# Products of the state with w_in as three float32r passes over split parts, two heads in halves of the array's rows

## The chip, the cores and the metric

One core of a Trainium2 chip. The metric is the device time of the kernel in microseconds (us), the median of several executions. Five engines matter here: PE (TensorE, matrix products; its weight loads are listed apart as PEld), ACT (ScalarE), DVE (VectorE), POOL (GpSimd) and SP, whose queue issues the transfers.

## The reference, cut to what matters

All tensors are float32.

```
x (8, 8, 512, 64), state (8, 8, 32, 64), w_in (512, 2048), w_out (2048, 512)
xread = softmax(x @ state^T / 8) @ state            # tokens read the state
sread = softmax(state @ x^T / 8) @ x                # the state reads tokens
X = concat(xread, sread) -> rows of batch and token, columns of head and D
h = X @ w_in ; g = max(0.01 h, h) ; Y = g @ w_out   # first feed-forward
out = (silu(Y @ w_gate) * (Y @ w_val)) @ w_out2     # second feed-forward
```

The kernel never forms xread. With A the softmax over the state, `xread @ w_in = A @ (state @ w_in)`, where the product in brackets is made per head: D = 64 rows of w_in belong to one head, so a tile of 128 rows holds a pair of heads. It is small, and it is needed before the first h.

## The kernel before, in words

The input weights arrive as 64-bit words and are converted to float32 in a **conversion** (`convert`, L236) that goes over 32 tiles of 128x512: 16 of w_in (key "in", g, k: column block g of 512, row block k, which is also the pair of heads) and 16 of w_out (key "out", f), in the order ORDER. One tile takes four chunks, each of which is one letter `c` of the scripts below; chunks of neighbouring tiles interleave. In an iteration for tile k the chunks are: (1) ACT `scale` of k, the ACT half of the split of tile k-2 (`finish1_h`, L1051), `limit` of k-1; (2) ACT `low` and DVE `sign` of k; (3) DVE `join` of k-1; (4) the DVE half of the split of k-2 (`finish1_l`, L1058), `add` of k-1, the load of a further tile, and a store of the tile k-1 to DRAM if it is one of w_in. `limit` and `add` are on DVE for the first four tiles and on POOL for the others. A **split** (L164 to L168) cuts a float32 tile into a float32r part h (ACT) and the rest l (DVE), so that a product at float32 accuracy is three fast passes, l*h, h*l and h*h (`passes`, L440). Before the change only w_out tiles are split here; a w_in tile is complete after its `add`, one iteration earlier.

Three things read a w_in tile. `product_sw` (L464): the pair's 64-row halves, two full float32 matmuls into two PSUM banks, with four batches of the state (`flat`) stationary; two ACT copies (L478) bring the banks to SBUF and two transfers store them, for the later batches. There are 32 of these, each a letter `p`. `state_win` (L455): batch 0 alone, 64 zero-padded columns of `states` per pair, two float32 matmuls into two halves of one bank, which are then split (`keep_sw_h`, `keep_sw_l`) for h at once. There are 8 of these; two are the letters `h` of START. The third reader is the store.

Work order is written out by hand, and each engine takes its instructions in that order. START is the script up to the first h: letters 0 and 1 step the two softmax chains of batch 0, s and S place the state (ACT copies, L1230), c is a chunk, p a product if a tile is ready, h and l the state_win of batch 0, m the first `h_mm`. SLOT0 has a script for each of the 16 slots of batch 0: in a slot there is one `h_mm` (6 matmuls), one `y_mm` (12 matmuls), some c and some p. From batch 1 on nothing of the conversion of w_in is left.

```
START = "spc0Scpccc0p0cpccpcc1ccchcc1cccpc1clcpp0hcccpclp1c01cpcmcc"
```

The PSUM banks of products: in START four of the pool ps_y; in SLOT0 the two banks a and b, one each, so that a second product in a row waits for the ACT copies of the first. `pump_until(key)` (L294) runs chunks until a tile is ready.

Of the kernel before, what the change touches and what calls it, by code (L numbers as in the profile page):

```python
# [25 lines left out]
def kernel(  # L26
# [39 lines left out]
    P = 128  # L66
# [141 lines left out]
    def to_f32(key):  # L208

        engine = nc.gpsimd if key[0] in ("in", "out") and key not in keys1[:4] else nc.vector  # L210
# [3 lines left out]
        v = raw[key].bitcast(I32)  # L214
        return {
# [20 lines left out]
    def convert(keys, room, prepare, load_next, finish=None):  # L236
# [4 lines left out]
        while todo or before or (finish and done):  # L241
# [209 lines left out]
    WO = {}  # L451
    products = []
    sw_ps, SW_raw, SW = {}, {}, {}
# [569 lines left out]
    with tc.manual_schedule():  # L1023
# [15 lines left out]
        pair = [None]  # L1039

        def place1(key):

            if key[0] == "in":
                n, half = divmod(KD * key[1] + key[2], 2)
                if half == 0:
                    pair[0] = wres.tile([P, 2, 512], F32, tag=f"wr{n + NF1 // 2}", name="w_in")
                raw[key] = pair[0][:, half, :]
            else:
                raw[key] = cv.tile([P, 512], F32, tag="raw", name="raw", bufs=4)

        def finish1_h(key):  # L1051
            while any((KD * g + p) // 2 + NF1 // 2 == key[1] for g, p, _ in products):
                pump_products(1)
            t = wres.tile([P, 2, 512], F32R, tag=f"wr{key[1]}", name="w_parts")
            WO[key[1]] = (t[:, 0, :], t[:, 1, :])
            split_h(t[:, 0, :], raw[key])

        def finish1_l(key):  # L1058
            split_l(WO[key[1]][1], raw.pop(key), WO[key[1]][0])

# [113 lines left out]
        def keep_steps(g, q):  # L1174
            def product():
                pump_until(("in", g, 2 * q + 1))
                keep_sw_h(g, q, state_win(0, g, q, "b"))
# [36 lines left out]
        flat = cv.tile([P, NPAIR, B, NS], F32, name="flat")  # L1214
# [9 lines left out]
        nc.gpsimd.memset(states, 0.0)  # L1224
        make_identity(nc, ident)
# [11 lines left out]
        for action in START:  # L1237
# [6 lines left out]
            elif action == "h":  # L1244
                keep_sw_h(*keep[0], state_win(0, *keep.pop(0), "y"))
# [4 lines left out]
            elif action == "S":  # L1250
                place_states(slice(1, B))
            elif action in "mM":
# [10 lines left out]
        for g, q in keep:  # L1263
            pump_until(("in", g, 2 * q + 1))
            keep_sw_h(g, q, state_win(0, g, q, "y"))
# [218 lines left out]
```

## Time and profile before

| | us |
|---|---|
| median of 3 runs (lowest to highest) | 1473.97 (1473.49 to 1474.21) |
| the profiled execution's own time | 1474.32 |
| its span in the trace | 1472.5 |
| PE busy in the span | 1445.5 |
| ACT busy / DVE busy | 688.4 / 817.5 |

The span starts with the first instruction and ends with the last; the execution's own time is 1.8 us more. Times in the rows are counted from the start of the span. In a list in order of time a row gives the start, the length, the engine, the line, the operation and its tiles, how many were merged, and in square brackets the idle time of the engine before it with what ended it.

### The profile page before, as it was taken

How to read it: one execution, taken by the hardware profiler on the slowest of the kernel's cores; microseconds unless marked ns; L12 is line 12 of the kernel's file. 1: busy time of each engine (PE TensorE's matmuls, PEld its weight loads, DVE VectorE, ACT ScalarE, POOL GpSimd, SP SyncE). 2: the span in 40 equal slices, each digit the busy share in tenths (PEclk: the TensorE clock that was granted, in tenths of full speed). 3: DMA queues.
4: the chain of work that ended last, by engine and by line, in shares of the span. 5: the costliest groups of instructions: out<-in, count | busy, mean ns of one | idle time of the engine just before them, and what ended most of it. 6: DMA issues, size and time to landing. Idle time of an engine off the chain costs nothing.

```text
span 1472.5 us, 20781 instructions
## 1 busy us (share of the span) xinstructions
PE 1445.5 (98%) x7530; PEld 1154.0 (78%) x7530; DVE 817.5 (56%) x1420; ACT 688.4 (47%) x1243; POOL 67.6 (5%) x64
## 2 busy tenths in 40 slices
PE   5989999999999999999999999999999999999998
PEld 1445777777777778888888888888888888988887
DVE  5666578676767676343444535455344555544442
ACT  5887556565656666444333423334233343333322
POOL 1565000000000000000000000000000000000000
PEclk9999999999999999999999999999999999999999
DMA  8886546666665655260668676667766397876345
GB/s 281 292 291 232 182 175 240 201 224 207 215 221 178 240 185 208 94 208 18 217 195 278 223 233 210 194 215 242 236 196 193 103 316 245 266 250 193 117 151 192
DMA packets 145766, 307.57 MB, mean 209 GB/s; under 512 B 14080, under 2 KB 34816, under 8 KB 144640
## 3 DMA queue, kind: packets, MB, share of 16 engines
q1 hardware_dynamic: 144368, 297.72, 61.6%
q10 hardware_dynamic: 1296, 8.52, 1.4%
q8 instruction: 60, 0.98, 0.3%
q14 instruction: 42, 0.34, 0.1%
HBM read 231.74 MB, written 74.45 MB: 208 GB/s over the span
## 4 chain that ended last, share of the span: by engine, by line
PE 93%; DMA 2%; ACT 2%; DVE 1%; issue 1%; POOL 0%; SPq 0%; ACTq 0%; POOLq 0%
PE ps_y L446 23%; PE ps_o L446 18%; PE ps_x L733 18%; PE ps_h L446 13%; PE ps_s L733 9%; PE ps_a L733 4%; PE ps_t L446 2%; PE ps_sw L470 2%; PE ps_yt L446 2%; PE ps_s L321 1%; DMA ws<-in_dram 1%; ACT sw L478 1%; PE ps_r L418 1%; DMA wo<-wo 1%; PE ps_a L404 0%
## 5 line engine op out<-in xcount | busy, mean ns | idle before, releaser
L446 PE MATMUL ps_y<-gh,w_parts 128*128 128x512 f32 x1024 | 339.3, 391 | 0.0
L733 PE MATMUL ps_x<-yc,wq 128*128 128x512 f32 x1152 | 278.0, 389 | 0.0
L733 PEld LDWEIGHTS ps_x<-yc,wq 128*128 128x128 f32 x1152 | 216.2, 188 | 44.8
L446 PE MATMUL ps_o<-wo,zh 128*128 128x512 f32 x768 | 236.4, 389 | 0.0
L446 PEld LDWEIGHTS ps_y<-gh,w_parts 128*128 128x128 f32 x1024 | 192.2, 188 | 51.6 <-issue 9.1
L446 PE MATMUL ps_y<-gl,w_parts 128*128 128x512 f32 x512 | 199.3, 389 | 0.0
L168 DVE TENSOR_TENSOR gl<-hs,gh 128x512 fp32r<-128x512 f32 (+1 forms) x144 | 99.2, 689 | 144.2 <-ACT gh L165 142.6
L446 PEld LDWEIGHTS ps_o<-wo,zh 128*128 128x128 f32 x768 | 144.1, 188 | 29.9
L541 ACT ACTIVATE hs<-ps_h 128x512 f32<-128x512 f32 (+1 forms) x144 | 82.6, 574 | 172.9 <-PE ps_h L446 169.1
L446 PE MATMUL ps_o<-wo,zl 128*128 128x512 f32 x384 | 149.5, 389 | 0.3 <-DMA wo<-wo 0.3
L733 PE MATMUL ps_s<-yc,wq 128*128 128x512 f32 x576 | 146.1, 389 | 0.0
L168 DVE TENSOR_TENSOR zl<-z,zh 128x512 fp32r<-128x512 f32 x96 | 66.3, 691 | 114.4 <-ACT zh L165 114.4
L733 PEld LDWEIGHTS ps_s<-yc,wq 128*128 128x128 f32 x576 | 108.1, 188 | 22.5
L165 ACT CAST zh<-z 128x512 fp32r<-128x512 f32 x96 | 59.3, 622 | 140.4 <-PE ps_o L446 140.3
L753 ACT ACTIVATE sg<-C 128x512 f32<-128x512 f32 x72 | 45.5, 632 | 158.2 <-DVE C L749 158.2
L446 PEld LDWEIGHTS ps_y<-gl,w_parts 128*128 128x128 f32 x512 | 96.2, 188 | 19.6
L446 PE MATMUL ps_h<-ah,swl 128*128 128x512 f32 x256 | 106.2, 415 | 1.6 <-DVE swl L168 1.5
L749 DVE TENSOR_TENSOR C<-ps_s,C 128x512 f32<-128x512 f32 x48 | 33.2, 691 | 123.3 <-PE ps_s L733 123.2
L446 PE MATMUL ps_h<-al,swh 128*128 128x512 f32 x256 | 100.2, 391 | 0.4 <-DVE al L168 0.4
L745 ACT COPY C<-ps_x 128x512 f32<-128x512 f32 x96 | 55.9, 583 | 94.6 <-PE ps_x L733 94.6
L446 PE MATMUL ps_h<-ah,swh 128*128 128x512 f32 x256 | 100.1, 391 | 0.0
L165 ACT CAST gh<-hs 128x512 fp32r<-128x512 f32 (+1 forms) x144 | 85.6, 594 | 3.0
(131 smaller groups left out, 1958.6 us busy)
## 6 DMA issues: line engine op xcount, KB each, us to landing
wo<-wo SPq DMA_DIRECT2D x96, 512.0 KB
wq<-quad_gate SPq DMA_DIRECT2D x168, 256.0 KB
wq<-quad_val SPq DMA_DIRECT2D x168, 256.0 KB
ws<-in_dram SPq DMA_DIRECT2D x68, 512.0 KB
sw<-sw_dram SPq DMA_DIRECT2D x56, 256.0 KB
quad_gate<-hl SPq DMA_DIRECT2D x24, 512.0 KB
quad_val<-hl SPq DMA_DIRECT2D x24, 512.0 KB
yr<-y_dram SPq DMA_DIRECT2D x34, 256.0 KB
```

Of the source, the lines that this page charges most:

```text
L165: nc.scalar.copy(dst, src)
L168: nc.vector.tensor_tensor(out=dst, in0=src, in1=hi.bitcast(F32), op=ALU.subtract)
L321: nc.tensor.matmul(ps[2 * NS * i:2 * NS * (i + 1)], lhsT=states[:, p, b, :], rhs=xt.pop((b, p)), start=True, stop=True,)
L418: nc.tensor.matmul(ps[NS * k:NS * (k + 1), i], lhsT=v["et"][:, n:n + NS], rhs=tokens[i][:, c, NS * k:NS * (k + 1)], start=(c == 0), stop=( ...
L446: nc.tensor.matmul(ps, lhsT=w, rhs=v, start=first and n == 0, stop=last and n == len(todo) - 1)
L470: nc.tensor.matmul(ps[e], lhsT=flat[half, p, 4 * bs:4 * bs + 4, :].rearrange("d b n -> d (b n)"), rhs=raw["in", g, p][half], start=True, s ...
L478: nc.scalar.copy(t, ps[e])
L541: nc.scalar.activation(hs, ps[:, :n], AF.Prelu, alpha=0.01)
L733: nc.tensor.matmul(bank, lhsT=a, rhs=v, start=first and n == 0, stop=last and n == len(todo) - 1, skip_group_check=True,)
L745: nc.scalar.copy(t[0], src)
L749: nc.vector.tensor_tensor(out=kept[0], in0=bank, in1=kept[0], op=ALU.add)
L753: nc.scalar.activation(t[0], c, AF.Sigmoid)
```

## The change

Each w_in tile is now split too. The converted float32 tile stays in one of four rotating buffers (`raw`, formerly only for w_out); its parts go to `WIN`, in places that w_out parts or an output tile use later (`places`), and before such a place is taken over, `clear` runs the products that still read it. A w_in tile is therefore ready one iteration of four chunks later, and `pump_until` stands before the `h` letters. The scripts START and SLOT0 are the same. The state is split as well (`split_states`, run at the letter S after the copies of the state): ACT half and DVE half of 128x1024, then 16 POOL copies of 64x32 into zero-padded columns for state_win, whose tile POOL clears at the start. `state_win` becomes six float32r matmuls over 128 rows and 128 columns; `product_sw` three pairs of float32r matmuls, the two 64-row halves alternating. Left out of the diff: a moved line and the tile allocations of `flat`.

```diff
                 load_next()
-                if not finish or before[0] == "in":
+                store(before)
+                if not finish:
                     ready.append(before)
-                    store(before)
...
-    def state_win(b, g, q, bank):
+    def state_win(g, q, bank):
         ps = (ps_y if bank == "y" else ps_a).tile([P, 512], F32, tag=bank, name="ps_sw")
-        for i in range(2):
-            nc.tensor.matmul(
-                ps[2 * NS * i:2 * NS * (i + 1)], lhsT=states[:, 2 * q + i, b, :], rhs=raw["in", g, 2 * q + i],
-                start=True, stop=True,
-            )
+        passes(
+            [((first_h[:, 2 * q + i], first_l[:, 2 * q + i]), w_parts(g, 2 * q + i)) for i in range(2)], ps, True, True
+        )
...
-        for e in range(2):
-            half = slice(D * e, D * (e + 1))
-            nc.tensor.matmul(
-                ps[e], lhsT=flat[half, p, 4 * bs:4 * bs + 4, :].rearrange("d b n -> d (b n)"),
-                rhs=raw["in", g, p][half], start=True, stop=True,
-            )
+        wh, wl = w_parts(g, p)
+        for n, (st, w) in enumerate(((flat_l, wh), (flat_h, wl), (flat_h, wh))):
+            for e in range(2):
+                half = slice(D * e, D * (e + 1))
+                nc.tensor.matmul(
+                    ps[e], lhsT=st[half, p, 4 * bs:4 * bs + 4, :].rearrange("d b n -> d (b n)"), rhs=w[half],
+                    start=n == 0, stop=n == 2,
+                )
...
+        places = ["y0", "y1"] + [f"wr{n}" for n in range(6, 16)] + ["y0", "y1", "wr14", "wr15"]
...
+        def finish1_h(key):
             if key[0] == "in":
+                t = win_tile(*key[1:])
+                WIN[key[1:]] = (t[:, 0, :], t[:, 1, :])
+                split_h(t[:, 0, :], raw[key])
+                return
...
+        def split_states():
+            split_h(flat_h, flat)
+            split_l(flat_l, flat, flat_h)
+            for t, of in ((first_h, flat_h), (first_l, flat_l)):
+                for p in range(NPAIR):
+                    for e in range(2):
+                        half = slice(D * e, D * e + D)
+                        c = NS * (2 * (p % 2) + e)
+                        nc.gpsimd.tensor_copy(out=t[half, p, c:c + NS], in_=of[half, p, 0])
...
             elif action == "h":
-                keep_sw_h(*keep[0], state_win(0, *keep.pop(0), "y"))
+                pump_until(("in", keep[0][0], 2 * keep[0][1] + 1))
+                keep_sw_h(*keep[0], state_win(*keep.pop(0), "y"))
...
             elif action == "S":
                 place_states(slice(1, B))
+                split_states()
```

## Rows read from the trace of the kernel before

**Rows 1.** The page: busy time, share of the span, instructions
```profile
PE 1445.5 (98%) x7530; PEld 1154.0 (78%) x7530; DVE 817.5 (56%) x1420; ACT 688.4 (47%) x1243; POOL 67.6 (5%) x64
```
**Rows 2.** Busy time by stretch (PE, PEld, DVE, ACT, POOL), granted clock, DMA share, GB/s
```profile
26.70:33.60 6.90, 6.18 (x12) 2.26 (x14) 5.47 (x13) 4.65 (x10) 1.90 (x2) 0.51 1.05 340
35.60:143.70 108.10, 100.00 (x361) 52.66 (x361) 72.79 (x107) 87.56 (x162) 61.73 (x53) 1.00 0.83 275
143.70:200.00 56.30, 56.30 (x311) 44.60 (x311) 34.93 (x69) 32.31 (x59) 0.00 (x0) 1.00 0.53 180
```
**Rows 3.** The tile ps_sw: its matmuls, and what its idle engine waited for (us, times)
```profile
L470 PE MATMUL ps_sw<-w_in,flat x128: 589/692/1219, 15.1 to 141.7; 64*128 64x512 f32 x128
...
  ACT sw L478: 19.8, 27
```
**Rows 4.** PE in order of time: a product and a state_win between h and y
```profile
40.67 0.39 PE L446 MATMUL ps_h<-al,swh 128*128 128x512 f32 x1
40.90 0.39 PE L446 MATMUL ps_h<-ah,swh 128*128 128x512 f32 x1
41.22 1.13 PE L470 MATMUL ps_sw<-w_in,flat 64*128 64x512 f32 x4
42.28 0.50 PE L446 MATMUL ps_y<-gh,w_parts 128*128 128x512 f32 x1
42.62 0.39 PE L446 MATMUL ps_y<-gl,w_parts 128*128 128x512 f32 x1
...
76.39 1.08 PE L458 MATMUL ps_sw<-w_in,states 128*64 128x512 f32 x4
77.39 0.50 PE L446 MATMUL ps_h<-ah,swl 128*128 128x512 f32 x1
```
**Rows 5.** PE in order of time: two products in a row
```profile
65.77 1.13 PE L470 MATMUL ps_sw<-w_in,flat 64*128 64x512 f32 x4
67.81 1.61 PE L470 MATMUL ps_sw<-w_in,flat 64*128 64x512 f32 x4 [0.91 <-ACT sw L478]
69.35 0.50 PE L446 MATMUL ps_h<-ah,swl 128*128 128x512 f32 x1
```
**Rows 6.** PEld in order of time: the weight loads of one product
```profile
41.22 0.30 PEld L470 LDWEIGHTS ps_sw<-w_in,flat 64*128 64x128 f32 x4 [0.35 <-issue]
```
**Rows 7.** DVE in order of time, in START
```profile
18.87 0.43 DVE L218 TENSOR_SCALAR w_in<-ws 128x512 int32<-128x512 int32 x1 [3.49 <-ACT ws L216]
37.10 0.69 DVE L168 TENSOR_TENSOR al<-a,ah 128x512 fp32r<-128x512 f32 x1 [0.86 <-ACT ah L165]
49.48 0.68 DVE L168 TENSOR_TENSOR w_parts<-raw,w_parts 128x512 fp32r<-128x512 f32 x1
50.08 0.68 DVE L168 TENSOR_TENSOR swl<-ps_sw,swh 128x512 fp32r<-128x512 f32 x1
```
**Rows 8.** ACT in order of time, in START
```profile
10.16 1.88 ACT L1230 COPY states<-flat 64x896 f32<-64x896 f32 x2
17.20 1.07 ACT L478 COPY sw<-ps_sw 128x512 f32<-128x512 f32 x2 [2.87 <-PE ps_sw L470]
34.96 0.62 ACT L165 CAST w_parts<-raw 128x512 fp32r<-128x512 f32 x1
35.47 1.08 ACT L478 COPY sw<-ps_sw 128x512 f32<-128x512 f32 x2
```
**Rows 9.** PE in order of time, in START: the first product and the first h
```profile
15.10 2.08 PE L470 MATMUL ps_sw<-w_in,flat 64*128 64x512 f32 x4 [5.45 <-DVE w_in L227]
35.62 0.49 PE L446 MATMUL ps_h<-ah,swl 128*128 128x512 f32 x1
```
**Rows 10.** The chain that ended last, pieces in order of time
```profile
80.27 2.08 DMA win_dram<-w_in
93.42 7.36 DMA ws<-in_dram
```
**Rows 11.** POOL in order of time, its first work on weights
```profile
24.60 1.01 POOL L221 TENSOR_SCALAR ws<-ws 128x512 f32<-128x512 f32 x1 [21.56 <-DVE raw L218]
```

More of the change, by code (lines that the diff above doesn't have):

```diff
@@ L208, in to_f32 @@
     def to_f32(key):
-        engine = nc.gpsimd if key[0] in ("in", "out") and key not in keys1[:4] else nc.vector
         t = staged.pop(key)
@@ L214, in to_f32 @@
         v = raw[key].bitcast(I32)
+        engine = nc.gpsimd if key[0] in ("in", "out") and key not in keys1[:4] else nc.vector
         return {
@@ L451, with w_parts @@
     WO = {}
+    WIN = {}
     products = []
+    kept = set()
     sw_ps, SW_raw, SW = {}, {}, {}
-    def state_win(b, g, q, bank):
+    def w_parts(g, p):
+        return WIN[g, p]
+    def state_win(g, q, bank):
         ps = (ps_y if bank == "y" else ps_a).tile([P, 512], F32, tag=bank, name="ps_sw")
-        for i in range(2):
-            nc.tensor.matmul(
-                ps[2 * NS * i:2 * NS * (i + 1)], lhsT=states[:, 2 * q + i, b, :], rhs=raw["in", g, 2 * q + i],
-                start=True, stop=True,
-            )
+        passes(
+            [((first_h[:, 2 * q + i], first_l[:, 2 * q + i]), w_parts(g, 2 * q + i)) for i in range(2)], ps, True, True
+        )
+        kept.add((g, q))
         return ps
@@ L1037, in next_load1, with win_tile, clear @@
                 stage(key, src, cv)
-        pair = [None]
         def place1(key):
-            if key[0] == "in":
[L1044 to L1055, printed above, removed]
+            raw[key] = cv.tile([P, 512], F32, tag="raw", name="raw", bufs=4)
+        places = ["y0", "y1"] + [f"wr{n}" for n in range(6, 16)] + ["y0", "y1", "wr14", "wr15"]
+        holds, y_place = {}, [None]
+        def win_tile(g, k):
+            place = places[KD * g + k]
+            clear(*(("y0", "y1") if place == "y0" else (place,)))
+            holds[place] = (g, k)
+            if place == "y0":
+                y_place[0] = ab.tile([P, 2, 2, 512], F32R, tag="yst", name="win_parts")
+            if place[0] == "y":
+                return y_place[0][:, int(place[1])]
+            return wres.tile([P, 2, 512], F32R, tag=place, name="win_parts")
+        def clear(*some):
+            for place in some:
+                one = holds.pop(place, None)
+                while one and any((g, p) == one for g, p, _ in products):
+                    pump_products(1)
+                assert not one or (one[0], one[1] // 2) in kept, one
+        def finish1_h(key):
+            if key[0] == "in":
+                t = win_tile(*key[1:])
+                WIN[key[1:]] = (t[:, 0, :], t[:, 1, :])
+                split_h(t[:, 0, :], raw[key])
+                return
+            f = key[1]
+            clear(f"wr{f}")
+            t = wres.tile([P, 2, 512], F32R, tag=f"wr{f}", name="w_parts")
+            WO[f] = (t[:, 0, :], t[:, 1, :])
             split_h(t[:, 0, :], raw[key])
         def finish1_l(key):
-            split_l(WO[key[1]][1], raw.pop(key), WO[key[1]][0])
+            parts = WIN[key[1:]] if key[0] == "in" else WO[key[1]]
+            split_l(parts[1], raw.pop(key), parts[0])
         keys2 = []
@@ L1176, in product @@
                 pump_until(("in", g, 2 * q + 1))
-                keep_sw_h(g, q, state_win(0, g, q, "b"))
+                keep_sw_h(g, q, state_win(g, q, "b"))
             return [{"P": [product]}, {"D": [lambda: keep_sw_l(g, q)], "cost": 0.6, "now": True}]
@@ L1212 @@
         low = list(keep)
-        flat = cv.tile([P, NPAIR, B, NS], F32, name="flat")
+        flat = ab.tile([P, NPAIR, B, NS], F32, tag="ah1", name="flat")
+        flat_h, flat_l = (cv.tile([P, NPAIR, B, NS], F32R, name=f"flat_{t}") for t in "hl")
+        firsts_hl = first1.tile([P, 2, NPAIR, P], F32R, tag="x_tail", name="firsts_hl")
+        first_h, first_l = firsts_hl[:, 0], firsts_hl[:, 1]
         for action in LOADS:
@@ L1224 @@
         nc.gpsimd.memset(states, 0.0)
+        nc.gpsimd.memset(firsts_hl.bitcast(F32), 0.0)
         make_identity(nc, ident)
@@ L1264 @@
             pump_until(("in", g, 2 * q + 1))
-            keep_sw_h(g, q, state_win(0, g, q, "y"))
+            keep_sw_h(g, q, state_win(g, q, "y"))
         for g, q in low:
```

## The prediction

> **What bounds the kernel now.** I read the page first, then the busy time by stretch, then the tile ps_sw, then each engine in order of time up to 145 us. Over the whole span PE is busy 98% [rows 1], but the change touches only work that ends at 142 us [rows 3]. From 143.7 us on PE has no gap, 56.30 us of 56.30 [rows 2], and none of that work changes, so the result is the time before plus or minus the shift of this point. Ahead of it are two stages. START, up to the first h at 35.62 us [rows 9], is a chain through DVE and ACT: the last softmax part (al) begins at 37.10 us [rows 7], PE mostly waits, and a stretch of it runs at a granted clock of 0.51, about 1.2 GHz [rows 2]; a product takes 2.08 us there [rows 9] and 1.13 us at the full clock [rows 4]. SLOT0, 35.6 to 143.7 us, has PE busy 100.0 of 108.1 us, ACT 87.56, DVE 72.79 and the DMA at 0.83 [rows 2]. PE's busy time there flatters: two products in a row should take 2.2 us and take 2.04 + 1.54, from 65.77 to 69.35 [rows 5], because the second waits for ACT to empty the banks; the idle time of engines ahead of ps_sw that ended with those copies is 19.8 us in 27 places [rows 3]. So in SLOT0 PE's work counts, and ACT's lateness counts almost as much.
>
> **A product, on PE.** It holds PE from 41.22 to 42.28, 1.06 us. The matmul ahead starts at 40.90 and would hold it 0.23 (the step from 40.67 to 40.90), which leaves 0.09 idle; the first matmul behind it takes 0.34 instead of 0.23 [rows 4]. The four records of the two halves lie in 1.13 us of which each takes 0.69 or 0.59 [rows 3, 4], and their four weight loads in 0.30 us [rows 6]: the halves run at the same time and load at the same time. The new product is three column passes of 512 where the old was four, in the same shape, so I take one pass off, 0.23 by the step between float32r matmuls, less a little for the additional pair of weight loads: **0.20 us saved**. No row shows a float32r matmul over 64 rows; the bounds are 0.23 (a whole step) and a loss of 0.46 if the halves did not overlap (6 x 0.23 + 0.14 = 1.52 against 1.06). START takes 28 product records before 35.62, which is 7 products; by the scripts one of its letters p no longer finds a ready tile, so 25 of the products of SLOT0 become cheaper, 25 x 0.20 = -5.0, and one is added there, +1.0 (0.86 and the 0.20 around it). Savings inside START lie beside the DVE chain and count nothing.
>
> **state_win, on PE.** Now 76.39 to 77.39, 1.00 us, and again 0.09 + 0.11 around it [rows 4]: 1.20. Then six matmuls of the same shape as their neighbours, 6 x 0.23 = 1.38. +0.18 each, six in SLOT0: **+1.1**.
>
> **START.** The chain through DVE, by the order of the instructions. (a) The state's copies leave ACT at 12.04 [rows 8]; the ACT half of 128x1024 is 1.1 us (0.94 for one 896-wide copy, times 1024/896), the DVE half 1.2 (two steps of 0.60 between 49.48 and 50.08 [rows 7]). DVE takes its instructions in order, so the first tile's sign and the first softmax steps, formerly done in a gap, wait until 14.4. Against that, the first p no longer finds a tile: ACT's wait of 2.87 us for that product [rows 8] goes, and with it DVE's wait of 3.49 us before 18.87 [rows 7]. By adding up, the sign that began at 18.87 begins at 19.2: +0.35. (b) Five DVE halves of splits (tiles 0 to 3, and 4, which comes ahead of al now) are in the chain: 5 x 0.60 = +3.0. (c) The first state_win waits for the split of tile 1, about 23.3; six matmuls at half speed are 2.8 us; its ACT copy stands in ACT's queue ahead of `scale` of tile 4, and that tile's sign, then the second softmax chain, stand behind it on DVE: about +2.9. Sum **+6.2**. Bounds: +2, if the idle times of DVE swallow most of it; +9, if PE, idle from 12 to 23 us, still has the low clock when the first 18 matmuls of h run (5.6 us at full speed). The 16 POOL copies cost nothing as long as POOL idles to 24.60 [rows 11].
>
> **ACT and DVE in SLOT0.** About 10 of the 16 w_in splits fall here. ACT: 0.51 each (34.96 to 35.47 [rows 8]), 5.1 us on an engine that is 81% busy and for which PE already waits; bounds 0 and 5.1, half taken: **+2.5**. DVE: 10 x 0.60 = 6.0 on an engine 67% busy; taken as hidden behind PE, +2 if not. In return the conversion is three chunks ahead at the end of START (pump_until runs them early), which takes one tile's scale and low off ACT and gives transfers, which had landed as much as 7.36 us after their issue [rows 10], a head start: -1.5. The four buffers `raw` now wait for the store of a w_in tile: 2.08 us in the chain [rows 10] against some 8 us (two and a half iterations of 108/32 us) until the buffer is written again, so nothing; with a store as slow as 7.36 still nothing, but DVE would stand in order behind a slower one, +3 at most.
>
> Sum: 6.2 - 5.0 + 1.0 + 1.1 + 2.5 - 1.5 = +4.3 on the profiled execution's 1474.3, which is 0.35 above the median: 1478.6 there, **1478** for the median.
>
> **Rivals.** First, the banks set the pace: a second product in a row waits for two ACT copies of about 0.53 [rows 8], not for PE, and with the splits in ACT's queue the copies come later. For it: 19.8 us [rows 3] and the pair of 3.58 us [rows 5]. Against it: most products stand alone between h and y. Then the -5.0 is gone and ACT's 5.1 counts whole: +11.9, 1486. The Trainium skill, TensorEngine Tiling, PSUM Bottleneck, has this as a rule: tiling the array speeds up the products and not the emptying of PSUM, which can then become the limit. By that rule the time would be this rival's. Second, on the faster side: the delay of START is swallowed. Its place is the DVE queue between 13 and 24 us; it decides if the first h comes less than 2 us later, because DVE's 3.49 us gap and the freed ACT pay for the splits. Then START is +1 and ACT's splits fall into its 20 us of idle time: 1 - 5.0 + 1.0 + 1.1 + 0 - 1.5 = -3.4, 1471. The trace is against it in that DVE is full from 18.87 on. Third, the change doesn't do what it says: the float32r halves run one after the other, 26 x (0.46 + 0.20) = +17 on the sum, 1495; the four loads in 0.30 us speak against it. Between the forecast and the second lies a mixture near 1474.
>
> **How the numbers follow.** 0.2% or 2.9 us is about what a measurement of this kernel can tell from no change. Forecast 0.50, with 1475 to 1482 as its own range (START +3 to +8): of it 0.13 lies within 2.9 us and 0.37 above. Banks 0.16, slower. START swallowed 0.20: 0.17 faster, 0.03 within. Halves in series 0.04, slower. Mixture 0.10, within, and 0.01 of it faster. Faster 0.18, same 0.25, slower 0.57. The range leaves out the third rival and the ends of the others: 1469.5 to 1487.
>
> **What would show it.** Right: the first h after 40 us, with DVE split rows of w_in in the chain; a product holding PE about 0.86 us with the halves' starts some ns apart; from 143.7 plus some 4 us on the same packed PE. START wrong: first h before 38. PE wrong: products of 1.4 us or more. ACT wrong: idle time ahead of ps_sw that ended with L478 well above 20 us, or well below. The prediction falls if DVE waits for stores into `raw`, or if the clock stays low after the first h.

## The result, and the profile after

The changed kernel takes **1492.34 us**, median of 4 runs (1491.35 to 1494.46), against 1473.73 us for the kernel before in the same session (4 runs, 1472.97 to 1474.21). The ratio is 1.0129, 95% interval 1.0111 to 1.0146. It is slower, as forecast, but by 18.6 us and not by 4, and so it lies above the range (1469.5 to 1487.0).

The profiled execution took 1492.35 us, its span is 1490.6. The page's busy times answer to [rows 1]: PE does as much as before (+0.7), ACT and DVE some 9 us more, POOL 9 more.

```profile
PE 1446.2 (97%) x7610; PEld 1169.2 (78%) x7610; DVE 825.9 (55%) x1437; ACT 697.8 (47%) x1260; POOL 76.2 (5%) x81
```

**START.** PE of the kernel after in order of time, the answer to [rows 9] and the first product behind START:

```profile
19.73 0.77 PE L446 MATMUL ps_sw<-win_parts,firsts_hl 128*128 128x512 f32 x1 [5.87 <-ACT win_parts L165]
...
23.40 1.22 PE L446 MATMUL ps_sw<-win_parts,firsts_hl 128*128 128x512 f32 x2 [0.37 <-DVE win_parts L168]
...
40.41 0.49 PE L446 MATMUL ps_h<-ah,swl 128*128 128x512 f32 x1
43.06 0.50 PE L446 MATMUL ps_h<-al,swh 128*128 128x512 f32 x1 [2.15 <-DVE al L168]
...
47.50 0.39 PE L446 MATMUL ps_h<-ah,swh 128*128 128x512 f32 x1
47.82 0.50 PE L478 MATMUL ps_sw<-win_parts,flat_l 64*128 64x512 f32 x2
48.16 0.63 PE L478 MATMUL ps_sw<-win_parts,flat_h 64*128 64x512 f32 x4
48.72 0.50 PE L446 MATMUL ps_y<-gh,w_parts 128*128 128x512 f32 x1
```

The first h starts at 40.41 us (before: 35.62), then PE waits 2.15 us for the softmax part al, and the last of the 18 h matmuls that come ahead of the first y is at 47.50 us (I count START to there); before it was at 40.90 [rows 4]. A product now holds PE from 47.82 to 48.72, 0.90 us; six matmuls one after the other would take 1.38 (6 x 0.23), so the halves run side by side. DVE of the same stretch, the answer to [rows 7]:

```profile
13.11 1.23 DVE L168 TENSOR_TENSOR flat_l<-flat,flat_h 128x1024 fp32r<-128x1024 f32 x1 [13.11 <-ACT flat_h L165]
...
19.21 0.43 DVE L218 TENSOR_SCALAR raw<-ws 128x512 int32<-128x512 int32 x1
...
42.35 1.45 DVE L168 TENSOR_TENSOR al<-a,ah 128x512 fp32r<-128x512 f32 x2
```

DVE's first instruction is the state's split half, at 13.11, and the work behind it in the queue waits. The softmax part that the second h matmul needs begins only at 42.35 and is done when that matmul starts, at 43.06.

**SLOT0.** To compare kernels I cut this stage at two matmuls that all of them have: from the 18th h matmul (the last of START) to the 96th. The kernel before, then the kernel after, with the columns of [rows 2]:

```profile
40.90:149.00 108.10, 100.51 (x368) 53.80 (x367) 72.97 (x106) 83.89 (x155) 59.38 (x52) 1.00 0.81 269
```

```profile
47.50:165.90 118.40, 102.98 (x435) 66.17 (x434) 76.79 (x116) 90.17 (x167) 58.34 (x49) 0.96 0.74 243
```

The stage is 10.3 us longer. PE idles 15.4 us in it (118.40 - 102.98) where it idled 7.6, and its granted clock is 0.96 where it was 1.00. The 96th matmul is 16.9 us late, and that is nearly the whole loss: at the 384th the kernels are 17.2 us apart, at the end of the spans 18.1. The tile ps_sw, the answer to [rows 3]:

```profile
L478 PE MATMUL ps_sw<-win_parts,flat_h x128: 386/393/789, 25.1 to 157.5; 64*128 64x512 f32 x128
...
  ACT sw L486: 43.2, 40
```

Ahead of products and state_win, engines idled 43.2 us until an ACT copy of a bank had ended (before 19.8). This sum counts PE and its weight loads apart and takes in START. PE's own waits from 40 to 165 us, before and after, by what it waited for (us, times, longest):

```profile
PE ps_sw L470 <- ACT sw L478: 4.4, 6, 0.9
PE ps_h L446 <- DVE swl L168: 1.5, 2, 1.0
PE ps_s L321 <- ACT sw L478: 1.4, 1, 1.4
```

```profile
PE ps_sw L478 <- ACT sw L486: 7.9, 9, 2.3
PE ps_h L446 <- DVE swl L168: 3.2, 2, 1.6
PE ps_sw L446 <- ACT sw L486: 2.1, 2, 1.6
```

With smaller rows (0.7 us for the copies, 0.7 for `swl`, 0.6 for parts of a tile), the waits for bank copies grow from 5.8 to 10.7 us and those for `swl`, DVE's half of the split of a state_win, from 1.5 to 3.9: about two thirds of the new idle time end with ACT's copies, and a third doesn't. One wait for a copy, in PE, then in ACT's queue, then as stretches with the granted clock:

```profile
97.88 0.63 PE L478 MATMUL ps_sw<-win_parts,flat_h 64*128 64x512 f32 x4
100.81 0.98 PE L478 MATMUL ps_sw<-win_parts,flat_l 64*128 64x512 f32 x2 [2.30 <-ACT sw L486]
```

```profile
97.60 0.67 ACT L216 ACTIVATE ws<-ws 128x512 f32<-128x512 f32 x1
99.17 0.62 ACT L165 CAST win_parts<-raw 128x512 fp32r<-128x512 f32 x1 [0.89 <-POOL raw L227]
99.69 0.59 ACT L549 ACTIVATE hs<-ps_h 128x512 f32<-128x512 f32 x1
100.18 1.06 ACT L486 COPY sw<-ps_sw 128x512 f32<-128x512 f32 x2
```

```profile
95.10:98.50 3.40, 3.40 (x19) 1.99 (x18) 3.07 (x5) 3.17 (x6) 2.37 (x3) 1.00 0.97 289
98.50:101.90 3.40, 1.10 (x8) 0.67 (x6) 2.21 (x3) 2.73 (x6) 2.52 (x3) 1.00 1.07 361
102.50:105.90 3.40, 3.40 (x10) 2.68 (x9) 2.72 (x4) 2.64 (x5) 1.38 (x2) 0.57 0.90 308
...
119.60:126.40 6.80, 6.06 (x17) 2.81 (x15) 2.62 (x5) 4.02 (x8) 1.75 (x2) 0.53 0.84 265
```

The split half of a w_in tile stands in ACT's queue at 99.17. It waits for POOL's `add` of that tile; `hs` and the two bank copies stand behind it, and the second product of a pair, for which PE was ready at 98.5, waits 2.30 us. The change added the cast, 0.62 us long and begun 0.89 us late; how much of the 2.30 us there would be without it, this trace alone can't say. A little later, PE runs at half the clock, 1.2 GHz: 3.4 us here, 6.8 us after 119.6. In the kernel before, nothing of this stage is below 1.00.

### The profile page after: what moved, and what is told of

Its sections match the earlier page's. It is cut to its first block, busy times and chain, and to the rows that moved or that the text cites. A ratio compares the mean times of both kernels' runs of the same rounds, so it can differ in the third digit from the quotient of the medians.

```text
span 1490.6 us, 20996 instructions
## 1 busy us (share of the span) xinstructions
PE 1446.2 (97%) x7610; PEld 1169.2 (78%) x7610; DVE 825.9 (55%) x1437; ACT 697.8 (47%) x1260; POOL 76.2 (5%) x81
## 4 chain that ended last, share of the span: by engine, by line
PE 90%; DMA 1%; DVE 0%; ACT 0%; issue 0%; ACTq 0%
PE ps_y L446 22%; PE ps_o L446 18%; PE ps_x L741 18%; PE ps_h L446 13%; PE ps_s L741 9%; PE ps_a L741 4%; PE ps_t L446 2%; PE ps_yt L446 2%; PE ps_s L321 1%; PE ps_r L418 1%; DMA wo<-wo 1%; PE ps_a L404 0%; PE ps_sw L478 0%; PE ps_sw L446 0%; PE ps_yt L571 0%; DVE ost L853 0%
## 5 line engine op out<-in xcount | busy, mean ns | idle before, releaser
L446 PEld LDWEIGHTS ps_y<-gh,w_parts 128*128 128x128 f32 x1024 | 192.9, 188 | 46.3 <-issue 5.1
L741 PEld LDWEIGHTS ps_s<-yc,wq 128*128 128x128 f32 x576 | 108.1, 188 | 22.5
L446 PE MATMUL ps_h<-ah,swh 128*128 128x512 f32 x256 | 100.5, 393 | 0.0
```

Of the source, the lines that this page charges most:

```text
L446: nc.tensor.matmul(ps, lhsT=w, rhs=v, start=first and n == 0, stop=last and n == len(todo) - 1)
L741: nc.tensor.matmul(bank, lhsT=a, rhs=v, start=first and n == 0, stop=last and n == len(todo) - 1, skip_group_check=True,)
```

## The experiments

The question is where the 18.6 us come from, above all the 10.3 us of SLOT0. Each quoted expectation names its theories by itself. To read the runs I use one ledger: START (the time of the last h matmul of START), the length of SLOT0 by the cut above, PE's idle time in it, the loss by the clock, and the rest, PE's work at full clock. The loss by the clock is PE's busy time in slices of 1.7 us, each times one minus the granted clock, summed. Each row is read from one profiled execution; each ratio is to the kernel before in the run's own session (medians of 1473.53 to 1474.33).

| kernel | median us | ratio (95%) | START ends | SLOT0 | idle | clock | work |
|---|---|---|---|---|---|---|---|
| before | 1473.73 | | 40.9 | 108.1 | 7.6 | 0.0 | 100.5 |
| after | 1492.34 | 1.0129 (1.0111 to 1.0146) | 47.5 | 118.4 | 15.4 | 4.8 | 98.2 |
| e1_splits_only | 1489.16 | 1.0100 (1.0085 to 1.0115) | 46.3 | 117.3 | 13.1 | 5.1 | 99.2 |
| e18_start_splits | 1479.10 | 1.0037 (1.0024 to 1.0050) | 45.8 | 108.0 | 7.4 | 0.0 | 100.6 |
| e2_products_only | 1472.97 | 0.9998 (0.9989 to 1.0008) | 39.7 | 106.9 | 10.7 | 0.0 | 96.2 |
| e16_both_products | 1474.23 | 0.9998 (0.9989 to 1.0007) | 40.4 | 108.1 | 10.3 | 1.7 | 96.1 |
| e15_start_freed | 1489.07 | 1.0100 (1.0085 to 1.0115) | 39.8 | 122.7 | 16.3 | 9.6 | 96.8 |
| e8_no_act_half | 1490.49 | 1.0109 (1.0094 to 1.0124) | 48.3 | 116.0 | 13.8 | 4.5 | 97.8 |
| e9_no_halves | 1487.41 | 1.0092 (1.0073 to 1.0110) | 48.9 | 113.8 | 11.9 | 4.5 | 97.4 |
| e19_pool_splits | 1499.72 | 1.0173 (1.0157 to 1.0188) | 50.3 | 124.0 | 16.9 | 10.0 | 97.1 |

### The splits alone, and the products alone

**e1_splits_only.** The kernel before, with the split of the state and of all w_in tiles into a spare tile that nobody reads; products, state_win and the time at which tiles are ready as before.

```diff
         def finish1_h(key):
+            if key[0] == "in":
+                n = len(extra) % 2
+                extra[key] = spare[:, 2 * n:2 * n + 2]
+                split_h(extra[key][:, 0], raw[key])
+                return
...
             elif action == "S":
                 place_states(slice(1, B))
+                split_states()
```

Left out of the cut: the DVE half in `finish1_l`, and `split_states`, which is that of the change.

> The kernel before, whose products and state_win stay float32, with the added splitting work alone: each w_in tile is split on ACT and DVE at the place where the change does it, into a spare tile that nobody reads; the state is split too, with its POOL copies. Tiles count as ready when they did before. Theory A (ACT and DVE work in their queues is the loss, in START and then in SLOT0): 8 to 14 us slower than before, 1482 to 1488. Rival B (the loss in SLOT0 comes from the forced products of the reused places and from the clock that falls in their wake): only part of START's delay is left, at most 5 us slower, below 1479. Rival C (the loss is the later readiness, one iteration of four chunks): about no change.

Measured: 1489.16 us, +15: just above the range of theory A, and far from B and C. The work of splitting alone costs four fifths of what the change costs, with float32 products unchanged. The wait shows as in the kernel after; PE and ACT of this kernel in order of time, then its stretches:

```profile
60.35 0.40 PE L447 MATMUL ps_y<-gh,w_parts 128*128 128x512 f32 x1
63.19 1.71 PE L471 MATMUL ps_sw<-w_in,flat 64*128 64x512 f32 x2 [2.44 <-ACT sw L479]
```

```profile
62.03 0.62 ACT L165 CAST spare<-w_in 128x512 fp32r<-128x512 f32 x1 [1.21 <-POOL w_in L227]
62.56 1.07 ACT L479 COPY sw<-ps_sw 128x512 f32<-128x512 f32 x2
```

```profile
59.80:63.20 3.40, 0.96 (x6) 0.44 (x4) 1.06 (x2) 2.19 (x5) 2.20 (x2) 1.00 0.76 292
63.20:70.00 6.80, 6.80 (x14) 3.09 (x14) 3.16 (x5) 4.36 (x8) 2.25 (x2) 0.50 0.68 200
46.30:163.60 117.30, 104.22 (x367) 56.10 (x366) 81.86 (x118) 90.48 (x168) 61.68 (x52) 0.96 0.73 248
```

Again a split's cast waits for POOL, the copies behind it come late, PE stands 2.44 us, and the next 6.8 us are at 0.50. This is not one place alone: PE waits 1.4 us or more for a copy at five places of this kernel's SLOT0, 9.0 us together (before 54.28, 63.19, 79.21, 86.55 and 102.12). At all five a cast of the added splits stands in ACT's queue ahead of the copies, and four of the five casts had themselves waited 0.83 to 1.27 us for POOL.

**e2_products_only.** The kernel before, with products as three pairs of float32r matmuls on one column of each tile, copied by POOL and spread over 512 columns, and without any split. The values of the products are left out.

```diff
+        w, st = tiny[:, 4 * g + p:4 * g + p + 1].to_broadcast([P, 512]), flat_r
+        for n in range(3):
+            for e in range(2):
...
+                    rhs=w[half], start=n == 0, stop=n == 2,
```

> The kernel before with product_sw alone as three pairs of float32r matmuls; nothing is split (the stationary side is a float32r copy of the state made early by POOL, the moving side one column of the tile, copied by POOL after the add and read 512 times, so that the wait for the tile stays; the values of these products are left out). Theory A: PE's saving of about 0.2 us on 25 products counts in SLOT0, 3 to 6 us faster than before, 1468 to 1471. Rival B says the same. Rival D (the two banks and ACT's copies set the pace of the products, so a cheaper product is worth nothing): within 2 us of before.

Measured: 1472.97 us, no difference that can be told from none (the interval goes from 1.6 us faster to 1.2 slower); rival D had this, theory A did not. PE's work in SLOT0 falls by 4.3 us (100.5 to 96.2, near the 5.0 of the sum), and 3.1 us of it come back as idle time. The profiled execution was one of the fastest of ten, its span 2.1 us shorter than that of the kernel before.

**e16_both_products.** As e2, and state_win as six float32r matmuls.

> The kernel before with both new forms on PE: products of the state as three pairs of float32r matmuls, and state_win as six float32r matmuls over 128 rows, all with one column of the tile (copied by POOL) spread over 512 columns; no splits of w_in, tiles ready as before. The values of both are left out. Theory A (the form costs PE little, the rest of the change brings the loss): state_win 1.2 us more in all than in the run with the products alone, 1473 to 1476 us. Theory B (the longer state_win, with ACT copies behind it, is a large part of the loss): 1479 us or more.

Measured: 1474.23 us, again no difference, as theory A had it. So the new forms on PE cost no time and gain none that these runs can tell. In the ledger 4.4 us less work come back as 2.7 us of idle time and 1.7 of lost clock.

### Which splits

**e18_start_splits.** As e1, but only the state and the four tiles of the first column block are split.

```diff
         def finish1_h(key):
+            if key[0] == "in" and key[1]:
+                return
```

> The kernel before with the extra work of START alone: the state split, and the four tiles of the first column block of w_in split into a spare tile that nobody reads; no split of the other w_in tiles, products and state_win as before. Nothing of the result is left out. Theory A (START's delay is worth what it moves the first h and its 18 matmuls, and is handed on unchanged): SLOT0 about 108 us long as before, 1477 to 1480 us. Theory B (the delay grows in SLOT0): SLOT0 113 us or longer, 1483 to 1489 us, near the run with all splits (1489).

Measured: 1479.10 us, +4.8, as theory A had it. START ends 4.9 us later, and SLOT0 is 108.0 us with 7.4 us idle and full clock, as before: the delay is handed on unchanged. Set beside e1, which differs from it by the split halves of 12 tiles alone, these cost 10.1 us. Their own time on ACT is 6.9 us and on DVE 9.0 (90.48 - 83.59 and 81.86 - 72.83 in these rows); PE's idle time grows by 5.7 and the loss by the clock by 5.1, less 1.4 of work. No wait of PE in this kernel's SLOT0 is longer than 1.25 us. PE's waits for the copies of products from 40 to 165 us in e1, then in this kernel, and this kernel's stretch:

```profile
PE ps_sw L471 <- ACT sw L479: 9.5, 7, 2.4
```

```profile
PE ps_sw L471 <- ACT sw L479: 4.5, 6, 1.0
```

```profile
45.80:153.80 108.00, 100.58 (x368) 53.87 (x367) 72.83 (x106) 83.59 (x155) 59.57 (x52) 1.00 0.80 269
```

**e15_start_freed.** The change, with START as light as before: the first block's tiles are not split, its products and state_win read one column (set in `place1`, left out of the cut), and POOL copies stand for the split of the state. The values of both are left out.

```diff
+                if finish and before[0] == "in" and before[1] == 0:
+                    nc.gpsimd.tensor_copy(out=tiny[:, before[2]:before[2] + 1], in_=raw[before][:, 0:1])
+                    ready.append(before)
...
-            split_h(flat_h, flat)
-            split_l(flat_l, flat, flat_h)
+            nc.gpsimd.tensor_copy(out=flat_h, in_=flat)
+            nc.gpsimd.tensor_copy(out=flat_l, in_=flat)
```

> The change with START freed: for the first column block (g = 0) the tiles of w_in are not split, their products and state_win read one column of the converted tile, copied by POOL and spread over 512 columns, and are ready as early as in the kernel before; the state's two split halves become POOL copies. SLOT0 is left as in the change. The values of the first column block and of the split of the state are left out. Theory A, the delay of START is worth its 6.6 us and no more: first h near 35.6 to 37 us, SLOT0 still about 118 us long, 1484 to 1487 us. Theory B, START's lateness also puts SLOT0 out of step (bunched products, low clock, later tiles): SLOT0 near 110 us, 1474 to 1481 us. If the first h stays at 40 us, the test is void.

Measured: 1489.07 us, above the ranges of both theories. START ends 7.7 us earlier than in the change, and only 3.3 us arrive: SLOT0 is 122.7 us long, with 9.6 us lost by the clock. With START as early as before, the whole loss is as large as e1's. One wait here is 4.06 us, and it is a w_out tile's cast that stands in ACT's queue; PE, then ACT:

```profile
118.04 1.28 PE L481 MATMUL ps_sw<-win_parts,flat_l 64*128 64x512 f32 x2 [4.06 <-ACT sw L489]
```

```profile
116.88 0.62 ACT L165 CAST w_parts<-raw 128x512 fp32r<-128x512 f32 x1 [2.04 <-POOL raw L227]
117.40 1.06 ACT L489 COPY sw<-ps_sw 128x512 f32<-128x512 f32 x2
```

**e8_no_act_half and e9_no_halves.** The change without the ACT half of the later blocks' splits (a constant stands for h), and without either half; the values of these products are left out.

```diff
+                if key[1]:
+                    WIN[key[1:]] = (flat_h.rearrange("p k b n -> p (k b n)")[:, 0:512], t[:, 1, :])
+                    return
...
+            if key[0] == "in" and key[1]:
+                WIN[key[1:]] = (parts[0], flat_l.rearrange("p k b n -> p (k b n)")[:, 0:512])
+                raw.pop(key)
+                return
```

> The changed kernel without the ACT half of the splits of the 12 w_in tiles of SLOT0 (column blocks 1 to 3): as the float32r part of these a constant part of the split state is read, so the values of their products are left out; the DVE half, the readiness, the places and the order are as in the change. START is untouched. Theory A (ACT's lateness, and the low clock that follows PE's waits): most of the 10 us that SLOT0 adds go, 1481 to 1486. Rival F (DVE's halves, or the readiness, cost as much): 1488 or more.

> As the run without the ACT half, and the DVE half of the same 12 tiles left out too. What stays of the change is START, the form of the products and the later readiness. Theory A: 1479 to 1484, START's 6 us and nothing more, at most 3 us below the run without the ACT half alone. Rival F: 4 us or more below that run.

Measured: 1490.49 and 1487.41 us, so 1.9 us and 4.9 us less than the change. Theory A, which had ACT's casts as most of the loss of SLOT0, is wrong here: without them 1.9 us come back of 10.3. Rival F held for e8; for e9 it asked for 4 us more, and 3.1 came. The 4.9 us are half of the 10.1 that the same splits cost in the kernel before: without them the change still has 4.5 us of lost clock and 11.9 us of idle time, and SLOT0 is 5.7 us longer than before. PE's waits for `swl` are as long in e9 (3.8 us) as in the change (3.9), where e1 has 1.1, so they don't come from these halves.

### Moving the splits

**e4_split_on_dve** puts the ACT half of w_in on DVE (`nc.vector.tensor_copy` in place of `split_h`); **e19_pool_splits** puts both halves of the later blocks on POOL.

```diff
+                if key[1]:
+                    nc.gpsimd.tensor_copy(out=t[:, 0, :], in_=raw[key])
...
+                nc.gpsimd.tensor_tensor(out=parts[1], in0=raw.pop(key), in1=parts[0].bitcast(F32), op=ALU.subtract)
```

> The changed kernel with the first half of each w_in split (the float32r part) on DVE instead of ACT. Takes 16 x 0.51 = 8 us from ACT, adds 16 x 0.35 to 0.6 us to DVE. Theory A (ACT's lateness in emptying the banks): 4 to 9 us faster than the changed kernel, 1483 to 1488, and the idle time of PE that ended with the copies of ps_sw falls from 43 us towards 25. Rival B (forced products, clock): within 3 us of the changed kernel. Rival E (DVE's chain in START is what counts): 2 to 5 us slower than it.

> The change, with both halves of the split of w_in on POOL for the 12 tiles of the later column blocks (about 24 instructions of 1 us or more on an engine that is busy 62 of 108 us there). Nothing is left out. Theory A (the splits cost by what they add to the queues of ACT and DVE, which empty the product's banks and make the softmax parts late): as good as leaving these splits out, 1486 to 1489 us, with the idle time ahead of the products no more than 37 us. Theory B (the tiles come later through POOL, products and state_win then wait for POOL): 1491 to 1496 us. If the gain of leaving the splits out was theirs on any engine, 1491 to 1493 us.

Measured: 1494.54 (1.0136, 1.0121 to 1.0152) and 1499.72 us. Neither helps. e4 is 2.2 us slower than the change, as rival E had it (and within rival B's 3 us): its START ends at 50.1 us instead of 47.5, and its SLOT0 is 117.4 us long, 1.0 less. e19 is above all three of its ranges: POOL was thought to have room; PE is idle for 16.9 us and the clock takes 10.0. One place in e19, where PE waits longest, by POOL, DVE, ACT and PE; last, ACT's waits for `add` ahead of w_out casts from 41 to 175 us (us, times, longest):

```profile
104.81 0.61 POOL L1077 CAST win_parts<-raw 128x512 fp32r<-128x512 f32 x1
105.39 0.64 POOL L221 TENSOR_SCALAR ws<-ws 128x512 f32<-128x512 f32 x1
105.99 1.29 POOL L1090 TENSOR_TENSOR win_parts<-raw,win_parts 128x512 fp32r<-128x512 f32 x1
107.97 1.33 POOL L227 TENSOR_TENSOR raw<-raw,ws 128x512 int32<-128x512 int32 x1 [0.69 <-DVE raw L224]
```

```profile
106.06 1.77 DVE L224 SCALAR_TENSOR_TENSOR raw<-ws,raw 128x512 int32<-128x512 int32 x1 [2.49 <-POOL ws L221]
```

```profile
109.33 0.62 ACT L165 CAST w_parts<-raw 128x512 fp32r<-128x512 f32 x1 [4.58 <-POOL raw L227]
109.85 0.61 ACT L165 CAST gh<-hs 128x512 fp32r<-128x512 f32 x1
110.37 0.66 ACT L217 ACTIVATE ws<-ws 128x512 int32<-128x512 uint32 x1
110.93 1.05 ACT L486 COPY sw<-ps_sw 128x512 f32<-128x512 f32 x2
```

```profile
112.13 1.19 PE L446 MATMUL ps_sw<-win_parts,firsts_hl 128*128 128x512 f32 x2 [4.54 <-ACT sw L486]
```

```profile
ACT w_parts L165 <- POOL raw L227: 11.6, 4, 4.6
```

POOL's cast stands ahead of `limit` of the following tile, for which DVE's `join` waits 2.49 us; the join then takes 1.77 us beside POOL's subtraction; `add` comes after it, the cast of that tile in ACT's queue waits for `add` 4.58 us, and PE waits 4.54 us for the bank copies behind that cast. ACT's waits for POOL's `add` are 11.6 us here; they are 5.1 us in the change (3.4 for w_out tiles, 1.7 for w_in) and 4.1 us before, in a window from 41 us on. Taking instructions off a queue doesn't help when what that queue waits for comes later.

**e12_copy_on_dve** (kernel before) and **e13_copy_on_dve_after** (change) put one of the two bank copies of each product on DVE.

```diff
-            nc.scalar.copy(t, ps[e])
+            nc.scalar.copy(t, ps[e]) if e == 0 else nc.vector.tensor_copy(out=t, in_=ps[e])
```

> The kernel before with the second of the two bank copies of every product on DVE instead of ACT, so that the two banks are emptied side by side. Theory D (the banks and ACT's copies set the pace of the products, which is why cheaper products alone were worth nothing): 3 to 8 us faster than before, 1466 to 1471. If DVE's queue is as late as ACT's: within 2 us, or slower.

> The changed kernel with the second bank copy of every product on DVE. Theory A and D: more than in the kernel before, 5 to 10 us below the changed kernel, 1483 to 1488, with the idle time of PE that ended with the copies well below 43 us. If DVE has no room for 32 copies of 0.6 us beside the splits: within 3 us or slower.

Measured: 1486.74 (1.0092, 1.0077 to 1.0107) and 1497.59 us (1.0163, 1.0148 to 1.0179). Theory D missed in both runs: the kernel before becomes 13 us slower, the change 5. In the kernel before START ends at 46.5 us instead of 40.9, and 4.8 us go to the clock in SLOT0. What DVE waits for most in this START (12 to 46.5 us) is new:

```profile
DVE sw L478 <- PE ps_sw L470: 3.8, 2, 2.2
```

The copies stand in DVE's queue and wait for PE's products, and the conversion and the softmax chain stand behind them. The Trainium skill, TensorEngine Tiling (Array Packing), PSUM Bottleneck, advises to empty PSUM with both ACT and DVE; here the measurement speaks against it. In this kernel an engine's busy share says little about the room in its queue: DVE was busy 73 of 108 us before this edit.

### The bunch of products, the state, the buffers

In the change, slot 6 has four products and not two, because `clear` forces two when a place is taken over. **e5_no_forced** gives the last two tiles other places; **e17_spread_p** puts a letter p more in slots 4 and 5; **e20_pool_spread** does that on top of e19.

```diff
-        places = ["y0", "y1"] + [f"wr{n}" for n in range(6, 16)] + ["y0", "y1", "wr14", "wr15"]
+        places = ["y0", "y1"] + [f"wr{n}" for n in range(6, 16)] + ["y0", "y1", "wr12", "wr13"]
```

```diff
-        "cDcHccApScYLcZpc",
-        "cccDHpccAccScpYLccZ",
+        "cDcHpccApScYLcZpc",
+        "cccDHpccApccScpYLccZ",
```

> The changed kernel with the last two w_in tiles in the places wr12 and wr13 instead of wr14 and wr15, whose products are done by then, so that no products are forced into slot 6. Theory A: within 3 us of the changed kernel, 1489 to 1495. Rival B: the four products in a row of slot 6 go, the clock stays up, and 6 to 10 us come back, 1482 to 1486.

> The change, with one letter p more in slot 4 and one more in slot 5, each alone between h and A, so that slot 6 has two products and not four (no product is forced there by the take-over of a place). Nothing is left out. Theory A (the bunch of four products in slot 6, each waiting for banks, costs some 2 to 4 us and lets the clock fall behind it): 1487 to 1490 us, the stretch of low clock near 120 us gone. Theory B (the bunch costs nothing of its own): 1491 to 1494 us.

> The same with the two letters p more in slots 4 and 5, so that no four products stand in slot 6. Nothing is left out. Theory A (with the splits off ACT and DVE there is room for the earlier products, and with the bunch gone the clock does not fall near 120 us): 1483 to 1487 us, below the run with the splits on POOL alone. Theory B (the letters only move the bunch, as in the run with the products spread, which was 2 us slower than the change): as much as the run with the splits on POOL alone, or 2 to 4 us more.

Measured: 1498.35 (1.0163, 1.0148 to 1.0179), 1495.96 (1.0137, 1.0117 to 1.0157) and 1500.42 us (1.0177, 1.0160 to 1.0194). No gain in any: e5 and e17 (1491.0 to 1497.0 in four executions) lie above both ranges of their theories, and theory B held for e20. In e5 the forced products stand five in a row behind 142 us, and the clock is low from 146.9 to 157.1; in e17 the stretch near 120 us is gone and others come, 9.8 us of lost clock in all instead of 4.8. The bunch is a place where the loss shows, and spreading it doesn't take the loss away.

**e6_state_later** moves `split_states` some chunks back in START, to the new letter k; **e7_warm_start** adds 16 matmuls in START and **e10_warm_slots** adds matmuls to SLOT0 (four ahead of the second product of a pair, six ahead of the h of three slots), into a bank that nobody reads; **e14_five_raw** gives `raw` five buffers.

```diff
-    START = "spc0Scpccc0p0cpccpcc1ccchcc1cccpc1clcpp0hcccpclp1c01cpcmcc"
+    START = "spc0Scpccc0p0cpcckpcc1ccchcc1cccpc1clcpp0hcccpclp1c01cpcmcc"
```

The matmuls of e7; those of e10 are the same in a helper:

```diff
+            ps = ps_h.tile([P, 512], F32, tag="h", name="ps_warm")
...
+                nc.tensor.matmul(ps, lhsT=w[:, 0:P], rhs=w[:, 0:512], start=True, stop=True)
```

> The changed kernel with the split of the state moved from the letter S to after the ninth chunk-letter of START, so that DVE's first conversions and the first softmax steps don't stand behind it. By the chain of DVE the first state_win and the first h come 2 to 4 us earlier (before 38.5 instead of 40.4 us). Theory A: the whole follows, 1488 to 1491. Rival G (SLOT0 takes its pace from elsewhere, the head start is swallowed): within 1.5 us of the changed kernel though h comes earlier.

> The changed kernel with 16 float32r matmuls over the split state added in START while PE idles (from about 13 us on; their result is not used), so that the granted clock has risen when the first state_win comes. If the low clock is the part (c) of START's delay that the prediction put there (2.8 us for a state_win at half speed, 1.4 at full): first h 2 to 3 us earlier, total 2 to 4 us below the changed kernel, 1488 to 1490. If DVE's chain alone sets START: first h unchanged, within 1.5 us.

> The changed kernel with matmuls added in SLOT0 where PE waits anyway: four float32r matmuls over the split state (into an idle bank of h, result not used) ahead of a product that follows another one directly, and six ahead of the h of slots 4, 8 and 12, which waits for DVE. Added PE work about 10 us, mostly inside waits of 1 to 2 us. Theory H (of the loss in SLOT0 4 to 5 us are the 10.2 us at half the granted clock): the low stretches at 103 and 120 us go, and the run is 1 to 5 us below the changed kernel, 1487 to 1491. Theory A alone (ACT's lateness, the clock only follows): the clock stays up but the time is the same or up to 5 us longer, since the added work delays PE.

> The changed kernel with five instead of four buffers for the converted tiles. Theory I (the conversion waits for the store of a w_in tile before its buffer is written again): 2 to 5 us below the changed kernel. By the waits in the trace of the changed kernel (POOL and DVE waited some 4 us in all for these stores, mostly off PE's path): within 1.5 us of it.

Measured: e6 1490.77 us (1.0113, 1.0097 to 1.0128), first h at 39.7 instead of 40.4; e7 1493.32 (1.0130, 1.0114 to 1.0147), first h at 41.7 but the last h matmul of START at 47.51, as in the change; e10 1491.34 (1.0119, 1.0102 to 1.0136), with as much lost by the clock as in the change, 4.8 us; e14 1492.37 (1.0126, 1.0111 to 1.0141). None moves more than 1.6 us from the change. e6's edit moved the first h by 0.7 us and not by 2 to 4, so it tests little. In e10 the added matmuls fill half of PE's idle time in SLOT0 (7.9 us are left of 15.4), but they didn't keep the clock up: it falls three times in the stage, and waits stayed. One stretch of 3.4 us and what follows it:

```profile
81.00:84.40 3.40, 1.63 (x8) 0.67 (x6) 0.69 (x2) 1.95 (x4) 2.21 (x2) 1.00 0.92 242
84.40:87.80 3.40, 3.40 (x10) 2.48 (x8) 2.61 (x5) 2.98 (x6) 1.27 (x1) 0.50 0.74 269
```

## Why the prediction was wrong in size

The sum forecast +4.3; the profile of the change has +16.9 at the 96th h matmul. By the prediction's own steps:

- **START, +6.2: right.** 6.6 us by the last h matmul of START (4.8 by the first, which now has a wait behind it). Term (a) held to the hundredth: the sign that began at 18.87 begins at 19.21 (forecast 19.2). For (b), five DVE halves of splits stand ahead of al, from 20.17, 22.67, 28.14, 31.48 and 38.18. For (c), the first state_win got its last part at 23.40 (forecast 23.3), PE ran it at a granted clock of 0.51, and the sign behind it waited 1.57 us for ACT's `scale`. What the clock had of (c) isn't shown: in e7 this state_win ran at the full clock, but its last part came 0.46 us later, and START ended as in the change. The 2.08 us of the first product [rows 9] are no example of the low stretch of [rows 2]: it runs at 15.10, where the profile's row says 1.00. e18 shows START's extra work alone at +4.8, handed on unchanged.
- **Products, 25 x 0.20, one more product, and state_win, together -2.9: right as PE's work, wrong as time.** A product holds PE 0.90 us (forecast 0.86), a state_win 1.36 (forecast 1.38), and PE's work in SLOT0 falls by 2.3. But e2, which has the whole gain and none of the cost, is not measurably faster (0.9998): 3.1 of its 4.3 us come back as idle time, 1.0 of it as waits for bank copies, 1.2 for `swl`. The rival named "the banks set the pace" had this step, and its sentence from the Trainium skill, TensorEngine Tiling (Array Packing), PSUM Bottleneck (tiling the array speeds up products and not the emptying of PSUM), agrees with e2 as far as idle time goes from 7.6 to 10.7 us while work falls from 100.5 to 96.2; but only a third of the new idle time waits for the emptying.
- **ACT and DVE in SLOT0, +2.5 and 0, with -1.5 for the conversion's head start, together +1.0: this step failed.** In its place stand 7.8 us of idle time (7.6 to 15.4) and 4.8 us by the clock, +12.6, of which some 3 are the saving on PE that came back (e2, e16). I bounded the casts by their own duration, 0 to 5.1 us, and called DVE hidden because it was 67% busy, with +2 if not. Added to the kernel before, the halves of 12 tiles cost 10.1 us (e1 against e18), above these 7.1: an instruction in a busy queue also costs what it waits for and what stands behind it, as the five places in e1 show. Taken out of the change, they give back 4.9 us, and ACT's alone 1.9 (e9, e8), inside the bounds. So the term was mis-sized for one kernel and not for the other, and the change has a second loss for which the sum had no term: without these halves SLOT0 is still 5.7 us longer than before (113.8), where the prediction had the conversion's new order at -1.5. No run measures that head start by itself.
- **The clock in SLOT0, no term: left out.** It takes 4.8 us. The prediction named a low clock as a sign of being wrong ("if the clock stays low after the first h"), but gave it no price in SLOT0. It came as separate falls, not as one that stays.
- **Stores into `raw`, 0: not contradicted.** A fifth buffer changes nothing (1492.37). In the change the trace puts one wait of POOL, 3.9 us, down to such a store; with five buffers it is still there (3.7).

The idle time that ended with L478's successor is 43.2 us, well above the 20 us that the prediction gave as the sign of "ACT wrong". The rival of the banks, 1486, was nearest: in e2 the -5.0 is gone, and in e1 the copies come later behind the splits. It is 6 us short; it too priced the splits by their duration and had no term for the clock.

Two things stay open. The parts are not additive: START freed gains 3.3 us of 7.7, and the later splits removed gain 4.9 of 10.1, so that the change without them (1487.41) is still 8 us above e18. Its pieces in the ledger are START (+3.1 us) and SLOT0 (+5.8: +4.5 idle, +4.5 clock, -3.2 work); whether the idle part comes from tiles that are ready an iteration later, from the forced products, or from the way in which these meet was not told apart. Part of it are PE's waits for `swl`, 3.8 us in e9 and 1.4 in e18; in e15, where START is freed, they are 1.5. No run has the later readiness alone. And no run removed only the wait of a cast for POOL, so its share was not measured: over the whole stage ACT waits 5.1 us for POOL's `add` in the change and 4.1 before, and PE's longest wait in e15 stands behind a w_out cast, which the kernel before has too.

No kernel here beats the kernel before; e2 and e16 equal it, with products whose values are left out.

## What to carry to other kernels

Price an instruction added to a busy in-order queue by what it waits for and by who stands behind it, not by its own duration alone: here 24 split halves of 0.6 to 0.7 us on ACT and DVE cost 10 us in one kernel, where the bound by duration was 7, and 5 in another, where other things were late as well. A faster product gained nothing here while what PE waits for kept its old pace; an experiment with the products alone shows that in one run. And where PE's waits grow in a stage at full clock, give the clock a term of its own.

## What the runs showed of the hardware

- In SLOT0 the granted clock fell to about 0.50 (1.2 GHz) behind stretches in which PE had waited: PE was busy 0.96 us of 3.40 in e1, 1.10 of 3.40 in the change, 1.63 of 3.40 in e10. The low stretches lasted 3.4 to 10.2 us (10.2 in e5 and e19). In the kernel before and in e18 it didn't fall in this stage. The longest single wait doesn't tell which it will be: the kernel before has one of 1.44 us, before 103.18, and keeps the full clock, while e16, whose longest is 1.15, has a low stretch of 3.4 us from 89.5.
- Pairs of float32r matmuls on the two 64-row halves run at the same time: three pairs hold PE 0.90 us, where two float32 matmuls of the same shape held it 1.06 [rows 4].
- POOL takes about 0.41 us for a 64x32 copy from the state's h part and 0.48 us from its l part (3.31 and 3.82 us for eight); 0.61 us for the cast of a 128x512 tile, as ACT does (0.62), but 1.29 us for the subtraction, for which DVE takes 0.69.
- DVE's `join` lasts longer while POOL subtracts: in e19 six of the 32 joins overlap POOL's subtraction by 1.19 to 1.22 us and take 1.74 to 1.77 us, the other 26 take 0.67 to 0.69.
